# Moving loads ahead of waits in a fused mLSTM and mixture-of-experts kernel: SP's order, POOL's queue and the last three units' product

## The chip, the cores and the metric

The kernel runs on one core of a Trainium2 chip. The metric is the device time of one execution in microseconds; lower is better. The core has a matrix engine (PE, with its weight loads PEld), a vector engine (DVE), a scalar engine for activations (ACT), a general engine (POOL), and SP, which here only issues DMAs. All DMAs are issued by SP or by POOL, each from a queue in program order: an instruction that waits holds back everything behind it on the same engine.

## The reference

Part one is an mLSTM over 4 batches, 8 heads, 768 steps and head size 40. Part two routes its 3072 output rows of 320 to the best 2 of 8 experts.

```python
for t in range(S):
    m_new = np.maximum(f_gate[:, :, t] + m, i_gate[:, :, t])
    f_stab = np.exp(f_gate[:, :, t] + m - m_new)
    i_stab = np.exp(i_gate[:, :, t] - m_new)
    C = f_stab * C + i_stab * einsum('bhd,bhe->bhde', vt, kt)
    n = f_stab * n + i_stab * kt
    h_tilde = einsum('bhde,bhe->bhd', C, qt)
    denom = np.maximum(np.abs(einsum('bhd,bhd->bh', n, qt)), 1.0)
    y[:, :, t] = sigmoid(o_gate[:, :, t]) * h_tilde / denom
...
noisy = x @ w_gate + log1p(exp(x @ w_noise)) * noise      # 8 logits a row
top2_w = softmax over the two largest
out[row] += top2_w[row, k] * (relu(x[row] @ w1[e]) @ w2[e])    # for both choices
```

## The kernel before

**Units.** The recurrence is computed by chunks of 64 steps. A unit is one chunk of two batches, 128 rows of x; there are 24 (`NU`): 12 chunks of the first two batches, then 12 of the others. The `while i < NU` loop holds one iteration a unit, in which the steps of several units are interleaved. For unit `u`: `e_part` makes the decay matrix `w` (PE, then Exp on ACT) from gate operands `LE` and `RE`; `s_part` multiplies queries and keys; `p_part` and `k_part` (DVE) weigh them (`p`, `kd`); `c_part` makes the next state, `o_part` the output; `f_part` divides by the normaliser on DVE (`tm`) and multiplies by the output gate on POOL (`XR[u]`, "xr" in the profile: the unit's 128 rows of x). An iteration later `t_part` transposes `XR` on PE for the router's logits.

**Loads.** `load_unit(u, "k")` brings queries and keys (tile `qk`, four buffers), `load_unit(u, "v")` values, keys and output gates (`vk`, four buffers), both from SP. In iteration `i` they are for unit `i + 3`. Its `vk` buffer is that of unit `i - 1`, so the load waits until `XR[i - 1]`, its last reader, is done. `keep_rows(i - 1)` writes `XR[i - 1]` to a table `rows` (`XD`) in DRAM: from POOL up to unit 11, from SP after. `gate_move` copies gate values into `LE` and `RE` every other iteration, from POOL for `i < XV` and from SP after. `piece_w1` and `early_w2` bring the first expert's weights in pieces.

**Routing.** Every four units form a group. The generator `g_part` picks the two experts of each row, their weights and their places; `fill` deals its steps out between the steps of the units. ACT's share of it is issued by `act()` at fixed points (L648). The step at L517 takes a difference `d` on POOL, which ACT then exponentiates; L549 and L550 give the two weights (`WTS`). Then their DMA to `rows` is put on the list `sent`, and SP issues it at the top of the next iteration (L762), or in `push()` behind the loop (L844). When the first 16 units are ranked, `decode` (L441 to L445) finds the rows of the first expert's first 512 places and `gather` (L716) fetches them and their weights from `rows` with four indirect DMAs on POOL, in the last iteration.

**Experts.** Behind the loop `transpose_x` (L746 to L750) turns each gathered tile: PE transposes, ACT and DVE split it into a high and a low part. Then `mm1` (L887) and `mm2` (L905 to L907) run for the two parts of each expert, and `put` adds the result to the output by indirect DMA. The output is first filled with zeros by 16 DMAs of SP (`zeros`, L275), and the second expert's weights follow them on SP.

The order on each engine is that of the program; nothing reorders it.

Of the kernel before, what the change touches and what calls it, by code (L numbers as in the profile page):

```python
# [17 lines left out]
NE, F, DM = 8, 1024, 320  # L18
# [3 lines left out]
NU = 2 * NCH  # L22
# [20 lines left out]
RW = 336  # L43

XV = 13
GC = 2
VW = 968
KE = 98
# [7 lines left out]
def build(ctx, tc, qk, vk, fi, noise, wgn, w1, w2, cst, ce, out):  # L56
    nc = tc.nc
    V, A, P, T, SP = nc.vector, nc.scalar, nc.gpsimd, nc.tensor, nc.sync
# [8 lines left out]
    XD = dram.tile([NTOK, RW], F32, name="rows")  # L67
# [9 lines left out]
    WTS = keep.tile([128, NU, RW - DM], F32, name="wts")  # L77
# [13 lines left out]
    gates = eg.enter_context(tc.tile_pool(name="gates", bufs=1, side="right"))  # L91
    RE = [gates.tile([128, 2, H, GC * L], FR, name=f"re{i}") for i in range(2)]
    LE = [gates.tile([128, GC, 192], FR, name=f"le{i}") for i in range(2)]
    HL = gates.tile([64, 2, S], FR, name="hl")
# [6 lines left out]
    SG = [t[:, 0, 648:VW] for t in VKS]  # L101
# [38 lines left out]
    def load_unit(u, what="kv", q=None):  # L140
        pr, c = divmod(u, NCH)
        if "k" in what:
            for p in range(2):
                (q or SP).dma_start(QK[u % 4][64 * p:64 * p + D], qk[pr, c, p])
        if "v" in what:
            flat = VKS[u % 4].rearrange("p x c -> p (x c)")
            SP.dma_start(flat[0:64, 0:VW], vk[pr, c, 0])
            SP.dma_start(flat[64:128, 648:648 + VW], vk[pr, c, 1])
# [56 lines left out]

    GB = NCH // GC

    def gate_move(kk, q=(SP, SP)):
        pr, k = divmod(kk, GB)
        j = kk % 2  # L210
        src = HL[32 * pr:32 * pr + 32, :, k * GC * L:(k + 1) * GC * L].bitcast(F32)
        q[0].dma_start(LE[j][64:96, :, 64:128].bitcast(F32), src[:, 0].rearrange("r (c t) -> r c t", c=GC))
        for x in range(2):
            q[x].dma_start(RE[j][96 + x:97 + x].bitcast(F32), src[16 * x:16 * x + 16, 1])

    def operands(j, p, eng=None):
        if p is None:
            A.activation(LE[j][0:KE], cet[0:KE, None, E_L:E_L + 192].to_broadcast([KE, GC, 192]), AF.Copy)
        else:
# [64 lines left out]
    W, PP, KD, SQ, OQ, XR, LG, MG = {}, {}, {}, {}, {}, {}, {}, {}  # L284
# [43 lines left out]
    def k_part(u):  # L328
        if u % NCH < NCH - 1:
            KD[u] = wk.tile([128, 2, H, D], F32, name="kd")  # L330
            V.tensor_mul(KD[u], VKS[u % 4][:, :, 328:648].rearrange("p x (h d) -> p x h d", h=H),
                         W[u][:, :, :, L - 1:L].to_broadcast([128, 2, H, D]))
# [29 lines left out]
    def f_part(u, step):  # L362
        ps = OQ[u]
        dn = wk.tile([128, H], F32, name="dn")
        V.tensor_scalar(dn, ps[:, :, D], 1.0, None, op0=OP.max)
        step()
        V.scalar_tensor_tensor(dn, ps[:, :, D], -1.0, dn, op0=OP.mult, op1=OP.max)
        step()
        V.reciprocal(dn, dn)
        step()  # L370
        XR[u] = rt.tile([128, DM], F32, name="xr", bufs=3)
        tm = wk.tile([128, H, D], F32, name="tm")
        V.tensor_mul(tm, ps[:, :, 0:D], dn[:, :, None].to_broadcast([128, H, D]))  # L373
        P.tensor_mul(XR[u], tm.rearrange("p h d -> p (h d)"), SG[u % 4])  # L374

    def keep_rows(u):
        (P if u < XV - 1 else SP).dma_start(XD[128 * u:128 * u + 128, 0:DM], XR[u])

# [91 lines left out]
    def g_part(g):  # L470

        u0, nb = GROUPS[g]
# [43 lines left out]
        d = sm("d", [128, nb])  # L516
# [32 lines left out]
        V.reciprocal(wt[:, :, 0], dd)  # L549
        P.tensor_mul(wt[:, :, 1], d, wt[:, :, 0])  # L550
        yield
        sent.append((XD.rearrange("(u p) c -> p u c", p=128)[:, u0:u0 + nb, DM:RW], WTS[:, u0:u0 + nb]))
        while not asked[4]:
            yield "wait"
        rank = rk[:, 8:].rearrange("p (e u) -> p u e", e=NE)
# [60 lines left out]
    sent = []  # L616
# [105 lines left out]
    def early_w2(j, n):  # L722

        SP.dma_start(raw2[:, j:j + n], w2[0, 128 * j:128 * (j + n)].rearrange("(j p) c -> p j c", p=128))
# [32 lines left out]
    i = 0  # L757
    while i < NU:
        unit[0] = i
        spent[0] = 0.0  # L760
        while sent:
            SP.dma_start(*sent.pop())  # L762
        if 1 <= i and i + 3 < NU:
            load_unit(i + 3)
        if i:
            keep_rows(i - 1)
        if i == 0:
            k_part(1)
        if i % 2 == 0 and i and i // 2 + 2 < 2 * GB:
            gate_move(i // 2 + 2, (P, P) if i < XV else (SP, SP))  # L770

        if W1LD <= i < W1LD + 12 and i % 2 == 0:
            j = (i - W1LD) // 2
            piece_w1(0, 512 * (j // 3), j % 3)
        if W2AT <= i < W2AT + 4:
            early_w2(2 * (i - W2AT), 2)
        if i == 3:
            SP.dma_start(cs[:, C_TRI:], cst[:, C_TRI:])
        if i == 4:
            SP.dma_start(nzt, noise)  # L780
        if not begun and done[0] >= E0U[0]:
            decode(0, E0S[1] // 128)
            begun = 1
        if begun and late < len(tiles(0, 0)):
            n = 2 if i + 1 < NU else 4
            gather(0, 0, tiles(0, 0)[late:late + n])
            late += n
            begun = 2
        if i == 0:
            sig_part(0)  # L790
        if i == 6:
            constants()
            V.tensor_copy(tri, cs[:, C_TRI:C_TRI + 128])
            V.tensor_copy(ones, cs[:, C_ONE:C_ONE + 128])
        if i + 1 < NU:
            p_part(i + 1)
        fill(0.2, False)
        if i + 2 < NU:
            s_room(i + 2)
        c_part(i)  # L800
        o_room(i)
        o_part(i)
        if i + LEAD < NU:
            e_part(i + LEAD, (0,))
        f_part(i, (lambda: fill(0.15, False)) if i + 2 < NU else (lambda: None))
        act()
        t = l_part(i)
        w = r_part(t)
        b = None if w else b_part(t)
        if i:  # L810
            t_part(i - 1)
            tc_part(i - 1)
        lc_part(i, t, w)
        bc_part(t, b)
        if i + LEAD < NU:
            e_part(i + LEAD, (1,))
        if i + 2 < NU:
            s_part(i + 2)
        fill(SHARE - spent[0])
        act()  # L820
        if i + 1 < NU:
            sig_part(i + 1)
        if i + 2 < NU:
            k_part(i + 2)
        fill(SHARE - spent[0])
        act()
        if i < 5:

            for _ in range(4):
                next(gates2, None)  # L830
        if W1AT <= i < W1AT + 12 and i % 2 == 0:
            next(pre1)
        if 6 <= i < 13:
            P.memset(XG[:, i - 6], 0.0)
        route(i)
        i += 1
        if i == NU - LEAD:
            eg.close()
            m1 = ctx.enter_context(tc.tile_pool(name="m1", bufs=1, side="right", reuse_waits="tile"))
            XH = m1.tile([128, 3, NT], FR, name="xh")  # L840
            XL = m1.tile([128, 2, NT], FR, name="xl")
# [341 lines left out]
```

## Time and profile before

| what | value |
|---|---|
| median of 3 runs | 570.92 us (570.37, 570.92, 576.92) |
| the profiled execution's own time | 572.61 us |
| its span in the profile | 570.5 us |
| mean granted clock of PE | 0.969 |
| the 24 units | about 7 to 142 us |
| from the last unit to the first expert's first product | about 142 to 152 us |
| the eight experts | about 152 to 564 us |

The span runs from the first instruction to the last; the rest of the execution's time lies around it. Rows of the profile give the start (or a count), a duration, the engine and line, the operation with the tiles it writes and reads, and in square brackets how long the engine had been idle just before and what ended that. "SPq" is SP's queue.

### The profile page before, as it was taken

Reading aid. Unit: us, or ns where it says so; the run is one execution under the profiler, and the core shown is the slowest. Engines: PE = TensorE matmul, PEld = TensorE weight load, DVE = VectorE, ACT = ScalarE, POOL = GpSimd, SP = SyncE. Lnnn points to the kernel's source line nnn. Section 1 sums busy time; section 2 is a strip of 40 time slices with the busy share of each in tenths; the row PEclk is TensorE's granted clock in tenths of the full one; section 3 lists DMA queues with packets and bytes.
Section 4 is the critical chain, followed back from the end, with each engine's and each line's share of the span. In section 5 each row is a group of like instructions: output and inputs, shape, how many; then the busy total and the mean of one; then the engine's idle time right before and its main releaser. Section 6 shows DMA issues by size and latency. Waiting matters only on the chain.

```text
span 570.5 us, 13345 instructions
## 1 busy us (share of the span) xinstructions
PE 545.3 (96%) x5158; PEld 494.8 (87%) x5158; DVE 352.4 (62%) x937; ACT 254.9 (45%) x621; POOL 244.0 (43%) x336
## 2 busy tenths in 40 slices
PE   8799898999699999999999999999999999999995
PEld 3588787888479898998899899889989998998995
DVE  8889999998594386654563565466356545644511
ACT  6576778876241354522541442254145225414500
POOL 7446676533456546046224604532460453241043
PEclk9799899998699899999999999999999999999998
DMA  5887889795379365264326326432642543232023
GB/s 142 190 212 209 210 203 219 213 236 152 105 235 312 85 114 128 93 152 71 114 42 146 90 93 149 63 99 59 150 96 93 143 58 85 79 40 25 2 31 47
DMA packets 41060, 71.11 MB, mean 125 GB/s; under 512 B 8761, under 2 KB 30478, under 8 KB 40992
## 3 DMA queue, kind: packets, MB, share of 16 engines
q1 hardware_dynamic: 29632, 51.23, 31.8%
q0 software_dynamic: 11360, 18.98, 19.3%
q8 instruction: 42, 0.69, 0.5%
q14 instruction: 26, 0.21, 0.1%
HBM read 52.76 MB, written 17.73 MB: 124 GB/s over the span
## 4 chain that ended last, share of the span: by engine, by line
PE 80%; DVE 8%; DMA 5%; ACT 3%; issue 2%; POOL 1%; SPq 1%; POOLq 0%; DVEq 0%
PE s L887 22%; PE e L887 11%; PE st L907 5%; PE st L906 5%; PE st L905 5%; PE o L907 4%; PE o L906 4%; PE o L905 4%; PE s L746 3%; PE s L323 3%; DMA vk<-vk_in 2%; PE o L360 2%; PE e L298 2%; PE st L351 2%; PE xt L405 1%
## 5 line engine op out<-in xcount | busy, mean ns | idle before, releaser
L931 POOL DMA_INDIRECT y_out<-y,tok x56 | 87.1, 1556 | 220.5 <-DVE y L921 219.8
L887 PE MATMUL s<-xh,w1h 128*128 128x512 f32 (+1 forms) x255 | 78.0, 361 | 1.5 <-DVE xh L750 0.9
L893 DVE SCALAR_TENSOR_TENSOR hlo<-s,hh 128x512 fp32r<-128x512 f32 (+1 forms) x85 | 47.4, 558 | 41.2 <-ACT hh L892 36.7
L748 ACT ACTIVATE xh<-s 128x384 fp32r<-128x384 f32 (+1 forms) x56 | 25.4, 469 | 103.2 <-PE s L746 102.9
L716 POOL DMA_INDIRECT xg<-rows,tok x56 | 58.4, 1043 | 26.2 <-issue 16.8
L892 ACT ACTIVATE hh<-s 128x512 fp32r<-128x512 f32 (+1 forms) x85 | 41.7, 491 | 48.6 <-PE s L887 46.5
L887 PE MATMUL s<-xh,w1l 128*128 128x512 f32 (+1 forms) x255 | 63.1, 356 | 0.0
L905 PE MATMUL st<-w2h,hh 128*128 128x320 f32 x184 | 58.0, 315 | 0.0
L907 PE MATMUL st<-w2h,hlo 128*128 128x320 f32 x184 | 57.2, 311 | 0.0
L906 PE MATMUL st<-w2l,hh 128*128 128x320 f32 x184 | 56.8, 309 | 0.0
L887 PEld LDWEIGHTS s<-xh,w1h 128*128 128x128 f32 x255 | 46.2, 190 | 7.9 <-ACT xh L748 2.0
L905 PE MATMUL o<-w2h,hh 128*128 128x320 f32 x168 | 53.0, 315 | 0.0
L907 PE MATMUL o<-w2h,hlo 128*128 128x320 f32 x168 | 52.4, 312 | 0.0
L906 PE MATMUL o<-w2l,hh 128*128 128x320 f32 x168 | 51.9, 309 | 0.0
L887 PEld LDWEIGHTS s<-xh,w1l 128*128 128x128 f32 x255 | 45.1, 190 | 6.0
L887 PE MATMUL s<-xl,w1h 128*128 128x512 f32 (+1 forms) x170 | 46.6, 355 | 0.5 <-DVE xl L749 0.5
L374 POOL TENSOR_TENSOR xr<-tm,vk 128x320 f32<-128x320 f32 x24 | 22.2, 926 | 43.0 <-DVE tm L373 12.9
L887 PE MATMUL e<-xh,w1h 128*128 128x320 f32 (+1 forms) x129 | 39.7, 363 | 0.0
L749 DVE TENSOR_TENSOR xl<-s,xh 128x256 fp32r<-128x256 f32 (+1 forms) x56 | 22.6, 404 | 26.9 <-ACT xh L748 23.3
L323 PE MATMUL s<-qk 64*64 64x64 f32 x768 | 36.2, 233 | 0.7 <-issue 0.7
L921 DVE TENSOR_SCALAR y<-st,gw 128x320 f32<-128x320 f32 x23 | 12.7, 551 | 39.2 <-PE st L907 39.2
L893 DVE SCALAR_TENSOR_TENSOR hlo<-e,hh 128x256 fp32r<-128x256 f32 (+1 forms) x43 | 23.8, 554 | 18.8 <-ACT hh L892 17.9
(203 smaller groups left out, 1368.7 us busy)
## 6 DMA issues: line engine op xcount, KB each, us to landing
vk<-vk_in SPq DMA_DIRECT2D x48, 242.0 KB
raw<-w_in SPq DMA_DIRECT2D x7, 1280.0 KB
qk<-qk_in SPq DMA_DIRECT2D x48, 160.0 KB
raw<-w_in SPq DMA_DIRECT2D x7, 1024.0 KB
y_out<-zrow SPq DMA_DIRECT2D x15, 320.0 KB
raw<-w_in SPq DMA_DIRECT2D x18, 256.0 KB
rows<-xr POOLq DMA_DIRECT2D x12, 160.0 KB
rows<-xr SPq DMA_DIRECT2D x12, 160.0 KB
```

The source lines that it names most:

```text
L323: T.matmul(SQ[u][:, p][half[p], h, :], q[r, 1, h, :], q[r, 0, h, :], start=True, stop=True)
L374: P.tensor_mul(XR[u], tm.rearrange("p h d -> p (h d)"), SG[u % 4])
L716: P.indirect_dma_start(out=XG[0:rows_of(t), t], out_offset=None, in_=XD[0:n], in_offset=bass.IndirectOffsetOnAxis(ap=token(e, t), axis=0), ...
L748: A.activation(XH[:, :, c], ps[:, :, 0:n], AF.Copy)
L749: V.tensor_sub(XL[:, :, c], ps[:, 0:2, 0:n], XH[:, 0:2, c].bitcast(F32))
L887: T.matmul(ps[:, 0:n], l, r, start=i == 0, stop=i == len(ops) - 1)
L892: A.activation(HH[:, f, c], ps[:, 0:m], AF.Relu)
L893: V.scalar_tensor_tensor(HLO[:, f, c], ps[:, 0:m], 0.0, HH[:, f, c].bitcast(F32), op0=OP.max, op1=OP.subtract)
L905: T.matmul(ps, HH[:, j, c], W2H[:, j], start=j == 0, stop=False)
L906: T.matmul(ps, HH[:, j, c], W2L[:, j], start=False, stop=False)
L907: T.matmul(ps, HLO[:, j, c], W2H[:, j], start=False, stop=j == 7)
L931: st = P.indirect_dma_start(out=out, out_offset=bass.IndirectOffsetOnAxis(ap=token(e, t), axis=0), in_=y[0:n], in_offset=None, compute_op= ...
```

## The change

Three things are changed. In an iteration SP issues the queries and keys first, then gates and weight pieces, and only then the values and the kept rows, which wait for x; where gates and kept rows go by POOL, they change places in the same way. The two weights of a group go to `rows` from POOL, where they are computed, instead of from SP's list. And the product that makes x runs on DVE instead of POOL for units 21, 22 and 23.

```diff
+XP = 21
...
-        P.tensor_mul(XR[u], tm.rearrange("p h d -> p (h d)"), SG[u % 4])
+        (P if u < XP else V).tensor_mul(XR[u], tm.rearrange("p h d -> p (h d)"), SG[u % 4])
...
         yield
-        sent.append((XD.rearrange("(u p) c -> p u c", p=128)[:, u0:u0 + nb, DM:RW], WTS[:, u0:u0 + nb]))
+        P.dma_start(XD.rearrange("(u p) c -> p u c", p=128)[:, u0:u0 + nb, DM:RW], WTS[:, u0:u0 + nb])
...
         spent[0] = 0.0
-        while sent:
-            SP.dma_start(*sent.pop())
         if 1 <= i and i + 3 < NU:
-            load_unit(i + 3)
-        if i:
-            keep_rows(i - 1)
+            load_unit(i + 3, "k")
         if i == 0:
             k_part(1)
         if i % 2 == 0 and i and i // 2 + 2 < 2 * GB:
...
         if W2AT <= i < W2AT + 4:
             early_w2(2 * (i - W2AT), 2)
+
+        if 1 <= i and i + 3 < NU:
+            load_unit(i + 3, "v")
+        if i:
+            keep_rows(i - 1)
```

**SP in iteration 14** (`qk`, `vk`: loads of unit 17; `rows<-xr`: kept rows of unit 13; `le`, `re`: gates; `raw`: a piece of weights). Before:

```order
L144 DMA qk_99<-qk_in 40x1024 x2
L147 DMA vk_103<-vk_in 64x968
L148 DMA vk_103<-vk_in 64x968
L377 DMA rows<-xr 128x320
L212 DMA le_93<-hl 32x2x64
L214 DMA re_91<-hl 1x16x128 x2
L117 DMA raw_113<-w_in 128x512
```

Now:

```order
L146 DMA qk_99<-qk_in 40x1024 x2
L214 DMA le_93<-hl 32x2x64
L216 DMA re_91<-hl 1x16x128 x2
L119 DMA raw_113<-w_in 128x512
L149 DMA vk_103<-vk_in 64x968
L150 DMA vk_103<-vk_in 64x968
L379 DMA rows<-xr 128x320
```

Gates and weights moved ahead of the values; the queries are behind the kept rows of the iteration before in both.

**POOL at the end of the loop** (`wts`: the weights of the group of units 12 to 15; `xr`: x of a unit; `xg<-rows`: the four gathers; `d`: the difference of the next group's logits). Before:

```order
L550 TENSOR_TENSOR wts<-d_2451,wts 128x4
L374 TENSOR_TENSOR xr<-tm,vk_102 128x320
...
L374 TENSOR_TENSOR xr<-tm,vk_103 128x320
L374 TENSOR_TENSOR xr<-tm,vk_104 128x320
L435 TENSOR_TENSOR tbl<-tbl,share 128x56
L716 DMA xg<-rows,tok 128x336 x4
L374 TENSOR_TENSOR xr<-tm,vk_105 128x320
L517 TENSOR_TENSOR d_2864<-mx_2827 128x4
```

Now:

```order
L552 TENSOR_TENSOR wts<-d_2451,wts 128x4
L554 DMA rows<-wts 128x4x16
L376 TENSOR_TENSOR xr<-tm,vk_102 128x320
...
L437 TENSOR_TENSOR tbl<-tbl,share 128x56
L718 DMA xg<-rows,tok 128x336 x4
L519 TENSOR_TENSOR d_2864<-mx_2827 128x4
```

The DMA of the weights stands between the weights and x of unit 20, and the three products of units 21 to 23 are gone from around the gathers.

**SP behind the loop** (`rows<-xr`: kept rows of units 22 and 23, in the second list of unit 21 too; `y_out<-zrow`: zeros; `rows<-wts`: weights of the last two groups). Before:

```order
L377 DMA rows<-xr 128x320 x2
L275 DMA y_out<-zrow 128x2x320 x2
L844 DMA rows<-wts 128x4x16
L275 DMA y_out<-zrow 128x2x320 x10
L844 DMA rows<-wts 128x4x16
L275 DMA y_out<-zrow 128x2x320 x3
L275 DMA y_out<-zrow 128x320
```

Now:

```order
L379 DMA rows<-xr 128x320 x3
L277 DMA y_out<-zrow 128x2x320 x15
L277 DMA y_out<-zrow 128x320
```

The two DMAs of weights between the zeros are gone, and the zeros stand directly behind the kept rows.

## The prediction

> **What bounds the kernel now.** I read the head of the page first, then busy time by stretch, then the waits.
>
> ```profile
> PE 545.3 (96%) x5158; PEld 494.8 (87%) x5158; DVE 352.4 (62%) x937; ACT 254.9 (45%) x621; POOL 244.0 (43%) x336
> ```
>
> The matrix engine (PE) is busy 96% of the span, so only its idle time and its slow-clock time can be won. The stretches (busy us of PE, PEld, DVE, ACT, POOL, then PE's granted clock, DMA share, GB/s) show where that lies:
>
> ```profile
> 54.00:66.00 12.00, 9.61 (x199) 8.60 (x193) 11.59 (x38) 7.20 (x18) 7.18 (x16) 0.86 0.80 209
> 82.00:90.00 8.00, 6.58 (x174) 5.78 (x172) 7.60 (x28) 5.84 (x16) 6.58 (x16) 1.00 0.88 208
> 90.00:125.00 35.00, 34.22 (x768) 30.14 (x765) 33.26 (x109) 27.97 (x71) 15.90 (x25) 1.00 0.85 214
> 125.00:132.00 7.00, 5.99 (x121) 5.13 (x116) 6.67 (x20) 5.29 (x14) 4.01 (x11) 0.82 1.00 269
> 142.00:152.00 10.00, 5.18 (x26) 3.40 (x26) 6.08 (x37) 3.43 (x11) 5.68 (x8) 0.73 0.47 145
> 158.00:166.00 8.00, 8.00 (x44) 6.74 (x43) 7.19 (x37) 2.30 (x8) 3.04 (x8) 1.00 0.92 309
> 190.00:540.00 350.00, 349.69 (x2130) 326.56 (x2131) 192.09 (x447) 136.30 (x336) 129.20 (x144) 1.00 0.41 91
> ```
>
> From 190 us on PE idles 0.3 us in 350, so nothing there can move. In the 24 units PE idles 2.4 + 1.4 + 0.8 + 1.0 = 5.6 us over the four early rows. The largest hole, 4.8 us, is 142 to 152, between the last unit and the first expert. What PE waits for in the units is told by the waits (us in total, times, longest):
>
> ```profile
> ACT d L648 <- POOL d L517: 13.4, 6, 4.8
> ...
> PE e L298 <- ACT w L301: 5.5, 4, 2.4
> ...
> PE e L298 <- DMA qk<-qk_in: 2.8, 1, 2.8
> ```
>
> PE waits for ACT's `w`, and ACT stood waiting for POOL's `d` (the routing), six times. Only one PE wait in the units is for a load, the early one; no row has PE waiting for a `vk` load.
>
> **The change, part by part.**
>
> *SP's order: 0.* SP does wait for x:
>
> ```profile
> SPq L147 <- POOL xr L374: 18.0, 8, 4.1
> ```
>
> But what it then issues has slack. The tightest `vk` load is unit 16's, used by the `kd` product on DVE; the slowest landing that the chain shows is 6.55 us:
>
> ```profile
> 89.26 0.47 SPq L147 DMA_DIRECT2D vk<-vk_in  x1
> 99.09 0.97 DVE L331 TENSOR_TENSOR kd<-vk,w 128x640 f32<-128x640 f32 x1
> 115.00 6.55 DMA vk<-vk_in
> ...
> 121.63 3.14 DMA vk<-vk_in
> ```
>
> 89.26 + 6.55 = 95.8 against 99.09: 3.3 us to spare, so an earlier load wins nothing. The queries now stand ahead only of their own iteration's gates and weights; they remain behind the previous iteration's `vk` load and kept rows, which wait for x. What can be lost: gates and weights now stand ahead of `vk`, 0.67 + 2.02 + 0.58 us of issue by these rows:
>
> ```profile
> 95.78 0.67 SPq L212 DMA_DIRECT2D le<-hl  x1
> 96.56 2.02 SPq L214 DMA_DIRECT2D re<-hl  x2
> 98.63 0.58 SPq L117 DMA_DIRECT2D raw<-w_in  x1
> ```
>
> These 3.3 us lie partly in the time in which SP waited for x anyway; even in full they just use up the slack above. I take 0 (bounds: 5.6 gained, if all of PE's idle time in the units hung on loads; 1 lost).
>
> *POOL's order up to unit 12: -0.3.* Gates now go ahead of the kept rows. In iteration 6:
>
> ```profile
> 51.87 0.59 POOL L377 DMA_DIRECT2D rows<-xr  x1 [0.30 <-POOL xr L374]
> ...
> 54.03 0.97 POOL L264 MEMSET w1l<- 64x1024 f32 x1
> ...
> 56.51 0.39 POOL L834 MEMSET xg<- 128x336 f32 x1
> 54.13 2.80 DVE L486 TENSOR_SCALAR t<-ue 128x32 f32<-128x32 f32 x1
> ```
>
> DVE's 128x32 operation stood 2.80 us, until POOL's row of memsets ended (56.90 against 56.93). It is what ACT's next logarithm waits for, and with it PE in the row 54 to 66. The kept rows waited 0.30 us for x just ahead; gates, which need no x, fill that. So POOL's row ends 0.3 us earlier: -0.3 (bounds -0.3 and 0).
>
> *The choices' weights by POOL: 0.* Six DMAs of 128 x 4 pieces of 64 bytes. No row shows one on POOL. Nearest are the kept rows, 128 pieces, and the gathers, 128 rows by index (min/median/max ns):
>
> ```profile
> L377 POOL DMA_DIRECT2D rows<-xr x12: 587/606/634, 25.8 to 85.4; - x12
> L716 POOL DMA_INDIRECT xg<-rows,tok x56: 941/1002/1307, 143.1 to 475.7; - x56
> ```
>
> The lower end is 0.61 us; the upper, at the gather's cost per piece, 4 x 1.00 = 4.0 us. I take 1.0, nearer the plain DMA, which it is. In the units it stands ahead of x (`xr`), which PE transposes later:
>
> ```profile
> 87.64 0.22 POOL L550 TENSOR_TENSOR wts<-d,wts 128x4 f32<-128x4 f32 x1
> 87.80 0.87 POOL L374 TENSOR_TENSOR xr<-tm,vk 128x320 f32<-128x320 f32 x1
> 91.33 0.52 PE L385 MATMUL xt<-cs,xr 128*128 128x128 f32 x3
> ```
>
> x then ends at 87.86 + 0.3 (the wait as at L377) + 1.0 + 0.87 = 90.0 against 91.33: hidden, with 1.3 us left. Its `vk` load, the one at 89.26 above, slips by about 1.3 us of its 3.3.
>
> The Trainium skill, page "SBUF — State Buffer", section "SBUF: two separate sides", speaks against this part: a DMA from POOL has its descriptors written there, and these are locked out while DVE runs an operation that takes the port pair they share. By it I should expect some of the six to stretch. The twelve kept rows span 587 to 634 ns in a stage with DVE at 33.26 of 35 us, so for DMAs the trace does not bear it out. By it the sum would grow only through case C below, and it is why C is not smaller.
>
> *x of units 21 to 23 by DVE, and what that frees: -0.5.* One such product is half of a `kd` (0.97 us at 128x640, above), so about 0.5 us; POOL's row of 0.87 is the upper end. Unit 22's falls into the 1.67 us in which DVE waited for `ue`. Units 21's and 23's push back routing work that PE reaches over 1 us later: 0, and 1.5 if none were covered. DVE's wait and POOL's tail before:
>
> ```profile
> 141.44 0.27 DVE L486 TENSOR_SCALAR t<-ue 128x32 f32<-128x32 f32 x1 [1.67 <-ACT ue L648]
> 143.05 1.16 POOL L716 DMA_INDIRECT xg<-rows,tok  x1 [1.39 <-DVE dn L365]
> ...
> 147.19 1.00 POOL L716 DMA_INDIRECT xg<-rows,tok  x1 [0.30 <-issue]
> 148.21 0.87 POOL L374 TENSOR_TENSOR xr<-tm,vk 128x320 f32<-128x320 f32 x1
> 149.27 0.20 ACT L648 ACTIVATE d<-d 128x4 f32<-128x4 f32 x1 [4.84 <-POOL d L517]
> ```
>
> The gathers start no earlier: POOL idled 1.39 us before the first, until DVE was past the decode of the places. But `d` loses the 0.87 us product ahead of it, and ACT and DVE turn to the first three tiles 0.8 us sooner. PE starts when the fourth has landed and been split:
>
> ```profile
> 147.19 2.99 DMA xg<-rows,tok
> 152.62 0.29 DVE L750 TENSOR_TENSOR xh<-s,xh 64x128 fp32r<-64x128 f32 x1
> PE s L887 <- DVE xh L750: 0.9, 1, 0.9
> ```
>
> DVE, behind by three tiles, finished the fourth at 152.91; the 0.8 us takes off 0.5 until the fourth tile itself is the limit. So -0.5 (bounds -0.9 and 0).
>
> *What follows on SP: +2.5.* SP's last kept row waited for POOL's late x; behind it stand the zeros for the output, 320 KB each:
>
> ```profile
> 140.88 8.57 SPq L377 DMA_DIRECT2D rows<-xr  x2
> 149.50 0.96 SPq L275 DMA_DIRECT2D y_out<-zrow  x2
> ...
> 158.06 7.94 SPq L275 DMA_DIRECT2D y_out<-zrow  x10
> 143.39 0.49 DVE L373 TENSOR_TENSOR tm<-o,dn 128x320 f32<-128x320 f32 x1
> ```
>
> Now x of unit 23 is ready at 143.9 + 0.5 = 144.4, and the zeros start at about 144.8 instead of 149.5; the weights, which held them back until 158, are gone from SP too. They are issued every 0.48 us but take 320 KB / 309 GB/s = 1.06 us each, so they pile up just while gathers two to four (144.5 to 148.2) need the DMA engines. Before, these had them alone. When the fourth is handed over, 7 are out: 7 x 1.06 - 3.4 = 4.0 us of zeros lie ahead. Bounds: 0, and +4.0 if it waits behind all. The nearest rows are the two `vk` landings, 6.55 against 3.14 us, +3.4 for a crowded one. I take +2.5, nearer to that than to 0 because gathers go by another queue.
>
> **Sum:** -0.3 - 0.5 + 2.5 = **+1.7 us**. On the profiled execution's 572.61 (a span of 570.5 and 2.1 around it) that is 574.3. That execution lay 1.7 above the median of the runs, 570.92, so the forecast for the median is **572.6**.
>
> **Rivals.**
>
> *A: the engines take gathers and zeros in turn.* Then a gather waits for at most one zeros DMA, 1.06 us: -0.8 + 1.06 = +0.3, or 571.2. For it: the two kinds come by different queues. Against: a `vk` load took 6.55 us where POOL's queue held little. No row of this trace shows a gather against a deep SP queue. The Trainium skill states A as a rule: in "DMA: Bandwidth & Descriptors", section "Queues, rings and completion order", each DMA engine goes round between the queues that have work, packet by packet.
>
> *B: loads did bound the units* by some wait put down to another engine. Then the 5.6 us of PE's idle time go: about 565.3. For it: SP's 18.0 us of waits for x. Against: 3.3 us of slack at the tightest load, and PE's stalls end on ACT.
>
> *C: the weights are dear on POOL* (slower). At 4.0 us, x of unit 12 ends at 93.0 and PE's transpose waits 1.7 us. At most four units have this: 6.8, so 579.4. It decides from 2.3 us a DMA on. Against: the 606 ns of 128 pieces.
>
> *D: SP's queue is not freed.* Queries still stand behind the previous kept rows; that is in the 0 above.
>
> **How the numbers follow.** Forecast (571 to 575) 0.45; A 0.27; B 0.08; C 0.12; 0.08 for what I do not see. The range 568.8 to 577.0 holds the forecast, A, and the cheap half of C. A measurement of this kernel tells about 2% (11.4 us) from no change. No case reaches that for certain: faster 0.02, same 0.95, slower 0.03.
>
> **What would show it.** Right: zeros issued from about 145, the fourth gather landing past 151.5, `d` on ACT at 148.5, PE's first expert at 153 to 155, the units' end within 0.5 us of before. Wrong: the fourth gather landing near 150.2 (A or better); `rows<-wts` on POOL over 2.3 us with PE waiting at L385's transposes (C); PE's idle time in the units gone (B).

## The result, and the profile after

The changed kernel takes **577.97 us** (median of 20 runs, 575.52 to 583.6) against 571.41 for the kernel before (20 runs beside it): a ratio of **1.0144, 95% interval 1.0121 to 1.0167**. This ratio leaves out, as slow, six executions of the kernel before (576.55 us and up) and none of the kernel after, so it lies above the quotient of the two medians, 1.0115. The forecast was 572.6 with a range up to 577.0. The profiled execution took 577.95, a span of 576.1; before it was 572.61 and 570.5.

Busy time by stretch of the kernel after (busy us of PE, PEld, DVE, ACT, POOL, PE's granted clock, DMA share, GB/s):

```profile
79.93:83.34 3.41, 1.66 (x64) 1.48 (x55) 3.27 (x20) 0.32 (x1) 0.90 (x3) 1.00 0.92 222
83.34:90.16 6.82, 6.82 (x79) 6.09 (x80) 5.68 (x16) 5.04 (x14) 6.08 (x12) 0.50 0.68 186
...
127.72:131.13 3.41, 2.00 (x32) 1.66 (x28) 3.27 (x10) 2.77 (x7) 1.61 (x5) 1.00 0.92 240
131.13:137.95 6.82, 6.65 (x102) 5.75 (x103) 5.56 (x15) 3.41 (x10) 3.73 (x7) 0.50 0.66 182
```

The same view of the kernel before:

```profile
83.34:90.16 6.82, 5.40 (x135) 4.67 (x133) 6.45 (x19) 6.00 (x16) 6.08 (x15) 1.00 0.88 212
...
126.09:129.50 3.41, 2.41 (x34) 1.84 (x34) 3.21 (x9) 3.25 (x10) 1.11 (x4) 1.00 0.98 276
129.50:132.91 3.41, 3.40 (x74) 3.11 (x68) 3.34 (x10) 1.83 (x5) 2.87 (x6) 0.50 1.08 258
```

PE's idle share tells nothing here: it is busy 95% and 96%. The clock column does. Between 80 us and the end of the units, PE after runs at half clock for two stretches of 6.82 us (79 and 102 matmuls where the full-clock stretch of before has 135); before, there is one of 3.41 us at 129.5. Each of these stretches follows one in which PE stood idle for 1 us or more. What made PE idle in the kernel after stands in its timeline (start, us, engine, line, out<-in, and in brackets the idle time ahead with what ended it):

```profile
78.66 1.27 POOL L139 TENSOR_TENSOR w1l<-raw,w1h 128x512 fp32r<-128x512 f32 x1 [1.02 <-ACT w1h L138]
78.69 1.29 DVE L505 TENSOR_TENSOR ln<-ln,nzt 128x32 f32<-128x32 f32 x1
...
83.34 0.55 PE L362 MATMUL o<-vk,p 64*64 64x41 f32 x6 [1.76 <-DVE tm L375]
...
123.05 1.31 POOL L139 TENSOR_TENSOR w1l<-raw,w1h 64x512 fp32r<-64x512 f32 x1 [1.07 <-DMA rows<-xr]
123.25 1.16 DVE L508 TENSOR_TENSOR nl<-ln,lg 128x32 f32<-128x32 f32 x1
131.28 0.80 PE L300 MATMUL e<-re,le 98*128 98x512 f32 x1 [1.56 <-ACT w L303]
```

and in that of the kernel before:

```profile
79.36 0.19 DVE L503 TENSOR_TENSOR ln<-ln,nzt 128x32 f32<-128x32 f32 x1
79.59 0.19 DVE L506 TENSOR_TENSOR nl<-ln,lg 128x32 f32<-128x32 f32 x1
80.05 1.29 POOL L137 TENSOR_TENSOR w1l<-raw,w1h 128x512 fp32r<-128x512 f32 x1 [1.74 <-ACT w1h L136]
```

A small DVE row of the routing, 0.19 us before, takes 1.29 and 1.16 us after: it starts 0.03 and 0.20 us behind POOL's split of `w1` and ends with it (78.66 + 1.27 = 79.93; 78.69 + 1.29 = 79.98). Before, the two rows were through 0.27 us ahead of the split. I call this a **collision**. From the second one to PE's wait the link is `d`: ACT stands for it longer than before, and the `w` that PE waits for stands behind it.

```profile
128.26 0.21 ACT L650 ACTIVATE d<-d 128x4 f32<-128x4 f32 x1 [2.76 <-POOL d L519]
```

Before:

```profile
125.84 0.21 ACT L648 ACTIVATE d<-d 128x4 f32<-128x4 f32 x1 [1.85 <-POOL d L517]
```

DVE rows stand beside POOL's product x as well, in the kernel before too (0.7 to 1.2 us); those are not counted here.

The end of the units and the hand-off to the experts, of the kernel after:

```profile
144.34 1.13 PE L362 MATMUL o<-vk,p 104*64 104x41 f32 x32
...
148.70 14.87 SPq L277 DMA_DIRECT2D y_out<-zrow  x16
150.99 1.00 POOL L718 DMA_INDIRECT xg<-rows,tok  x1 [0.30 <-issue]
...
156.28 0.90 PE L748 MATMUL s<-cs,xg 128*128 128x128 f32 x3 [0.20 <-DMA xg<-rows,tok]
157.77 0.79 PE L890 MATMUL s<-xh,w1h 128*128 128x512 f32 x1 [0.58 <-ACT xh L750]
```

and the same matmuls of the last unit before:

```profile
140.51 1.13 PE L360 MATMUL o<-vk,p 104*64 104x41 f32 x32
```

The last unit's `o` matmuls start at 144.34 (before 140.51) and the first expert matmul at 157.77 (151.70). So of the 5.6 us of span, **3.8 arise in the units, 2.2 in the hand-off** (13.4 us against 11.2), and -0.4 behind it.

### The profile page after: what moved, and what is told of

Its sections match the earlier page's. It is cut to its first block, busy times and chain, and to the rows that moved or that the text cites. A ratio compares the mean times of both kernels' runs of the same rounds, so it can differ in the third digit from the quotient of the medians.

```text
span 576.1 us, 13332 instructions
## 1 busy us (share of the span) xinstructions
PE 546.1 (95%) x5158; PEld 495.7 (86%) x5158; DVE 357.7 (62%) x940; ACT 255.0 (44%) x621; POOL 246.3 (43%) x339
## 4 chain that ended last, share of the span: by engine, by line
PE 74%; DVE 12%; DMA 6%; ACT 3%; issue 2%; POOL 2%; SPq 1%; POOLq 0%; DVEq 0%
PE s L890 22%; PE e L890 10%; PE st L910 5%; PE st L909 5%; PE st L908 5%; PE o L910 4%; PE o L909 4%; PE o L908 4%; PE s L748 3%; DMA vk<-vk_in 2%; DVE p L339 2%; DVE ob L604 2%; PE s L325 1%; PE o L362 1%; PE o L916 1%
## 5 line engine op out<-in xcount | busy, mean ns | idle before, releaser
L376 POOL TENSOR_TENSOR xr<-tm,vk 128x320 f32<-128x320 f32 x21 | 21.0, 1000 | 36.0 <-DVE tm L375 13.8
L909 PEld LDWEIGHTS st<-w2l,hh 128*128 128x128 f32 x184 | 34.9, 189 | 0.0
```

The costliest lines, as they stand in the source:

```text
L376: (P if u < XP else V).tensor_mul(XR[u], tm.rearrange("p h d -> p (h d)"), SG[u % 4])
L909: T.matmul(ps, HH[:, j, c], W2L[:, j], start=False, stop=False)
```

## The experiments

Four marks are read from each profile, in us: the start of the last unit's `o` matmuls (**units' end**); PE's **half clock** from 80 us to there; the **gathers**, from POOL's first gather to PE's first expert matmul; and where a **collision** starts. The half clock ahead of 80 us is left out: besides a stretch in the first units, between 14 and 33 us, it is the one near the wait at 57 to 60 us that all kernels have, which was 3.4 to 13.7 us long behind the same code (3.4 in both before and after); so the units' end of one profile is good to some 5 us. Ratios are to the kernel before on the same chip.

| run | ratio (95%) | median us | units' end | half clock | gathers | collisions |
|---|---|---|---|---|---|---|
| before | 1 | 569.7 to 572.1 | 140.5 | 3.4 | 8.65 | none |
| after | 1.0144 (1.0121 to 1.0167) | 577.97 | 144.3 | 13.6 | 10.9 | 78.7, 123.3 |
| p1_order | 1.0066 (1.0014 to 1.0118) | 571.1 | 138.5 | 3.4 | 8.8 | none |
| p2_weights | 1.0179 (1.0097 to 1.026) | 578.3 | 145.0 | 10.2 | 8.5 | 121.9 |
| p3_x_dve | 1.0013 (0.9969 to 1.0058) | 570.0 | 137.9 | 0 | 9.5 | none |
| c1_weights_sp | 0.9993 (0.9944 to 1.0043) | 571.6 | 136.9 | 0 | 10.0 | none |
| a2_held | 1.011 (0.9987 to 1.0233) | 580.1 | 147.5 | 13.6 | 10.4 | 127.9 |
| c2_zeros_free | 0.9996 (0.9943 to 1.0049) | 570.7 | 137.3 | 0 | 9.7 | none |
| d3_free | 1.0015 (0.9973 to 1.0057) | 572.1 | 137.9 | 0 | 10.5 | none |
| d2_held | 1.0023 (0.9978 to 1.0067) | 570.2 | 141.2 | 0 | 8.5 | none |
| d1_behind | 1.0104 (1.0062 to 1.0147) | 578.4 | 144.2 | 13.6 | 8.6 | 78.7, 123.1 |
| d4_after_behind | 1.0159 (1.0083 to 1.0234) | 581.5 | 146.4 | 17.1 | 10.5 | 78.4, 123.4 |
| e2_dve_twice | 1.0048 (1.0011 to 1.0084) | 572.8 | 139.9 | 3.4 | 9.1 | none |
| e3_dve_else | 1.0162 (1.0114 to 1.0211) | 577.2 | 147.2 | 6.8 | 8.75 | 103.9 |
| f1_guard | 1.0115 (1.0063 to 1.0167) | 576.3 | 139.8 | 3.4 | 10.7 | none |
| f2_held_guard | 1.0002 (0.9969 to 1.0036) | 570.8 | 137.7 | 0 | 8.55 | none |

Four more runs move the splits and stand below.

### Each part alone

Order alone: the diff of the change from `load_unit(i + 3, "k")` on, with `sent` left in place.

> The kernel before with one part alone: in a unit SP and POOL get queries, gates and expert weights first, then the v rows and the kept rows; choices' weights stay on SP, x stays on POOL. Theory T (the units' +3.8 us are a matter of phase: the order shifts DVE's routing work against POOL's low parts of w1, a two-input DVE row then stands about 1.1 us behind a 1.28 us POOL row, PE runs dry and goes to half clock): the last unit's o matmuls start 2 to 5 us later than the 140.5 of before or about the 144.3 of after, with rows of 1.0 to 1.3 us at L503 or L506 beside the low parts at L137; time about +2 to +5 us. Rival R1 (the weights' DMA on POOL makes x late, and with it the routing): this part alone has no such DMA, so the units end at 138 to 140.5, the time is 0 to -2 us. Rival R2 (gates ahead of v rows make loads late): like T in time, but PE's or DVE's waits in units 11 to 13 and 20 to 22 end on vk loads. The hand-off (last o matmuls to PE's first expert matmul, 11.2 us before, 13.4 after) stays at 11.2 in all of them.

Weights alone:

```diff
-        sent.append((XD..., WTS[:, u0:u0 + nb]))
+        P.dma_start(XD..., WTS[:, u0:u0 + nb])
```

> The kernel before with one part alone: the choices' weights by POOL's queue. The DMA takes 0.8 to 0.85 us there as in the kernel after. Theory T: no change of order ahead of unit 8, so the early 2.2 us are not won; POOL's rows move by about 1 us from unit 8 on, a collision may come or go: -1 to +2 us in the units. Rival R1: the units lose 3 to 5 us, with PE waiting for transposes of x or for routing behind them. Hand-off: the last group's weights no longer stand ahead of the zeros on SP, but the zeros still wait for x of unit 23 on POOL (149 us): 11.2 us, or up to 12 if the zeros that follow without a pause reach the fourth gather.

x alone:

```diff
-        P.tensor_mul(XR[u], ...)
+        (P if u < 21 else V).tensor_mul(XR[u], ...)
```

> The kernel before with one part alone: x of units 21 to 23 by DVE. Units as before up to unit 21 (last o matmuls at 140.5, within 0.5 us). Hand-off: x of unit 23 about 4 us earlier, so two zeros DMAs start at about 145, and the rest still waits for the last group's weights on SP: theory T (zeros ahead of the gathers cost the hand-off 2.3 us when 7 or more are out): two zeros are 2.1 us of transfers issued ahead of three gathers, so 10.5 to 12 us; total -0.5 to +1 us. Rival R3 (the hand-off's loss comes from DVE's products and the changed order on POOL, not from zeros): 13 us or more, total +2 us.

x costs nothing that the comparison tells, the order 0.1 to 1.2%; **the weights alone bring a loss as large as the whole change's** (578.3). Theory T had put it on the order, and falls; R1 had the part right. In the timeline and the stretches of the run with the weights alone the link is the same as after:

```profile
121.88 1.27 POOL L137 TENSOR_TENSOR w1l<-raw,w1h 64x512 fp32r<-64x512 f32 x1 [1.01 <-DMA vk<-vk_in]
121.91 1.28 DVE L503 TENSOR_TENSOR ln<-ln,nzt 128x32 f32<-128x32 f32 x1
130.29 0.49 PE L298 MATMUL e<-re,le 98*128 98x512 f32 x1 [1.55 <-ACT w L301]
```

```profile
132.28:142.52 10.24, 10.22 (x165) 9.30 (x161) 7.63 (x19) 5.16 (x12) 2.69 (x6) 0.50 0.33 100
```

One collision, PE idle for 1.55 us instead of 1.00, and 10.24 us at half clock where before had 3.41. The extra 6.8 us at half speed are 3.4 us, and the longer wait 0.55: most of the 4.5 us by which its units end later than before's. That the longer wait made the stretch longer is not shown by one profile each.

### The weights undone in the changed kernel

```diff
-        P.dma_start(XD..., WTS[:, u0:u0 + nb])
+        sent.append((XD..., WTS[:, u0:u0 + nb]))
...
+        while sent:
+            SP.dma_start(*sent.pop())
```

> The kernel after with one part undone: the choices' weights go by SP again, as before. Theory W (formed from the parts alone: the weights' DMAs on POOL, 0.8 us each ahead of x, put DVE late; its routing rows then fall behind POOL's split of w1, PE runs dry, and the clock goes to half for multiples of 3.4 us): without them no DVE row at L505 or L508 over 0.3 us, half clock in the whole span 27 us as before (37.6 after), last o matmuls at 137.5 to 140.5 (144.3 after), hand-off 11 to 11.8 us since the last group's weights hold the zeros; time within 1.5 us of before. Rival Q (the parts cost together what none costs alone: the new order and x on DVE together): last o matmuls past 143, time +4 us or more.

As W expected, but for a hand-off of 12.6 us in place of 11 to 11.8 (two zeros stood ahead of the gathers); the parts do not cost more together. In its timeline DVE is through 0.4 us ahead of the split, PE's wait is 0.47 us, and there is no half clock from 80 us to the units' end:

```profile
118.57 0.19 DVE L508 TENSOR_TENSOR nl<-ln,lg 128x32 f32<-128x32 f32 x1
119.16 1.27 POOL L139 TENSOR_TENSOR w1l<-raw,w1h 64x512 fp32r<-64x512 f32 x1 [1.12 <-DMA rows<-xr]
125.63 0.49 PE L300 MATMUL e<-re,le 98*128 98x512 f32 x1 [0.47 <-ACT w L303]
```

### The zeros

> The kernel before with x of units 21 to 23 by DVE, and the weights of the last group alone by POOL, the other five groups' by SP. Its units are those of the run with x on DVE alone (last o matmuls 137.9, within 1.5), but nothing holds the zeros on SP after x. Theory Z (zeros ahead of the gathers): hand-off from the last o matmuls to the first expert matmul 13 to 13.8 us, against 11.0 to 11.5 where the zeros came late or only two came; fourth gather 5 us from its issue to the transpose; time +1.5 to +4 us against x on DVE alone. Rival R3 (the long hand-off comes with the weights' DMAs or the order of the units): 11 to 11.8 us.

> The kernel after, with the weights of the last group alone by SP again, so that they hold all but two zeros DMAs behind the hand-off; the other five groups' weights by POOL. Units as after (last o matmuls 143 to 145.5). Theory Z: hand-off 11 to 11.8 us in place of 13.4, time about 2 us under after (575 to 576.5). Rival R3: hand-off stays at 13 us or more, time as after.

Both edits (the weights of the last group alone by another queue than the rest) missed their aim: the group ahead of the last also comes behind the units. So c2 still had two zeros ahead of the fourth gather, a2 five. Done properly, with x of units 21 to 23 on DVE as in c2:

```diff
+        if u0 < 16:
             sent.append(w)
+        else:
+            P.dma_start(*w)
```

> The kernel before with x of units 21 to 23 by DVE, and the weights of the last two groups by POOL, which both come behind the units; in the earlier run only the last group's were, and those of the one ahead of it still held all but two zeros. Units as with x on DVE alone. Theory Z: five zeros or more ahead of the fourth gather, first gather to first expert matmul 10.4 to 11 us, time +1 us against x on DVE alone, 0 to +2.5 against before. Rival R3: 9.5 to 10 us as with two zeros.

and the opposite, no zeros ahead, again with x on DVE:

```diff
-        mm1(0, 0, f, wipe)
+        mm1(0, 0, f, wipe if f else lambda: None)
```

> The kernel before with x of units 21 to 23 by DVE, and no zeros asked for in the first of the eight steps, so that all of them stand behind a group's weights, which come at about 155 us. Theory Z: with no zeros ahead of the gathers the first gather to the first expert matmul takes 8.0 to 8.4 us (9.5 with two zeros, 8.65 in before, where x and its product stand ahead of the routing on POOL), time 1 us under x on DVE alone, -0.5 to -2 us against before. Rival R3 (DVE's product and POOL's order make the hand-off long, not the zeros): 9.5 us or more, no gain.

Over the runs of the table, the gathers' mark goes by the zeros issued before POOL is through with issuing the fourth gather: none, 8.5 to 9.1 us (eight runs); two, 9.5 to 10.0 (three); five, 10.4 to 10.9 (five). It does not go by who multiplies x or sends the weights, so theory Z stands and R3 falls. The fourth gather and its transposition in d3, then in d2, whose zeros start at 158.02:

```profile
141.78 14.74 SPq L275 DMA_DIRECT2D y_out<-zrow  x16
...
144.03 0.99 POOL L720 DMA_INDIRECT xg<-rows,tok  x1 [0.30 <-issue]
...
148.98 0.90 PE L750 MATMUL s<-cs,xg 128*128 128x128 f32 x3 [0.35 <-DMA xg<-rows,tok]
```

```profile
147.26 1.00 POOL L716 DMA_INDIRECT xg<-rows,tok  x1 [0.30 <-issue]
...
150.16 0.90 PE L746 MATMUL s<-cs,xg 128*128 128x128 f32 x3 [0.17 <-DMA xg<-rows,tok]
```

From issue to transposition it is 4.95 us with the zeros and 2.90 without.

In the total, neither differs from before by more than the comparison tells.

### Where the weights' DMA stands on POOL

The DMA behind the group's last small product on POOL, so that x no longer waits for it: on the kernel before (d1) and on the changed one (d4).

```diff
         P.tensor_mul(OVM[:, u0:u0 + nb, 2:4], wt, ov)
+        P.dma_start(XD..., WTS[:, u0:u0 + nb])
```

> The kernel before with the choices' weights by POOL, as in the run with that part alone (578.3 us, +8.5), but the DMA issued behind POOL's last small product of the group (L586 of before) in place of ahead of x. POOL has the same DMAs, x no longer waits for them. Theory X (the cost is x being 1.1 us late on POOL, so that DVE's routing rows stand until the late product of x ends): DVE's rows are stretched by 9.5 to 11 us in all between 56 and 146 us, as before (10.6; 12.2 with the DMA ahead of x), last o matmuls at 137 to 141 (145.0), time within 1.5% of nothing: -1 to +2 us against before. Rival P (any DMA of 0.8 us on POOL in a routing group costs as much, by what it keeps from POOL or by descriptors that shut DVE out): last o matmuls 143 to 146, time +5 us or more.

> The kernel after with the same move: the weights' DMAs behind the group's last small product on POOL, all else as after; the zeros on SP stay free. Theory X with theory Z: last o matmuls 136 to 140 (144.3 after), first gather to first expert matmul 10.4 to 11 us as after (10.9; 8.5 to 8.8 where no zeros stand ahead), time -1 to +2 us against before. Rival P: last o matmuls past 143, time +5 us.

X falls, P holds: 578.4 and 581.5. But the rows of d1's timeline are again a collision, and PE's waits are those of the kernel after to 0.01 us (1.76 and 1.56):

```profile
122.90 1.30 POOL L137 TENSOR_TENSOR w1l<-raw,w1h 64x512 fp32r<-64x512 f32 x1 [0.34 <-DMA vk<-vk_in]
123.09 1.15 DVE L506 TENSOR_TENSOR nl<-ln,lg 128x32 f32<-128x32 f32 x1
```

### The splits of w1 moved

`a1_odd`: all six in odd units; `c3_late_split`: ACT's and POOL's part of the second and sixth one unit later; `e1_low_late`: POOL's part alone of these two; `e4_held_low_late`: the same as e1, on d2, without weights on POOL.

```diff
-        if W1AT <= i < W1AT + 12 and i % 2 == 0:
+        if W1AT < i < W1AT + 12 and i % 2:                            # a1
+        if i in (8, 11, 12, 14, 16, 19):                              # c3
+        if W1AT <= i < W1AT + 12 and i % 2 == 0 or i in (11, 19):     # e1, e4
...
+                if lo is P and (f, k) in ((0, 1), (512, 2)):              # e1, e4
+                    yield
                 lo.tensor_sub(W1L[n, k, s], ...)
```

> The kernel after, with the six splits of w1 in odd units (9 to 19) in place of even ones (8 to 18); the routing's two-input DVE rows stand in even units. Theory T: no row at L505, L508 over 0.3 us, PE's stalls in units 12 to 13 and 21 shrink to those of before or less, no half-clock stretch at 84 to 90; the last o matmuls start at about 139 to 141.5 in place of 144.3, the time falls by 3 to 5 us against after, to about -1 to +4 us against before with the hand-off of 13.4 us unchanged. Rivals R1 and R2 (late x, late loads): the stalls stay, the last o matmuls start at 143.5 to 145, the time stays within 1 us of after's 576.4 to 578.

> The kernel after, with the second and the sixth split of w1 one unit later (units 8, 11, 12, 14, 16, 19 in place of 8, 10, 12, 14, 16, 18): the two that stood beside DVE's L505 at 78.7 us and L508 at 123.3. Theory W with the collision as its link: no such row over 0.3 us, PE's idle 1.76 us at L362 gone, half clock in the units 17 us down to 7 to 10, last o matmuls at 139 to 142 unless the moved splits meet other rows of DVE (over 0.6 us beside L139). Rival W2 (the weights' DMAs cost by x being late, the split has no part in it): last o matmuls stay at 143.5 or later.

> The kernel after, weights' DMAs and all, with POOL's low part of the second and the sixth piece of w1 one unit later (units 11 and 19), while ACT's high part stays where it was (the earlier run moved both, and put 0.61 us of ACT's work between d and w). Theory K (collision: the two-input routing rows of DVE stand behind the split): no row over 0.3 us at L505 or L508 of after, PE's idle before the o matmuls of unit 12 1.0 us or less (1.76), half clock in the units 10 us or less (17), last o matmuls at 137 to 141 (144.3), time -0.5 to +3 us against before with the hand-off of after. Rival P (the DMAs on POOL cost by themselves): last o matmuls past 143, time +5 us or more.

> The kernel before with x of units 21 to 23 by DVE, all zeros behind the weights (the run with the shortest hand-off), and POOL's low part of the second and the sixth piece of w1 one unit later. Theory K: fewer executions in which the rows collide, so fewer runs above 573 us (14 of 29 of before's last runs); median 568 to 570.5, -0.5 to -3 us against before. Rival (the upper runs of before have another cause): same share of runs above 573, median as before.

All four take longer than before: 1.0211 (1.0114 to 1.0307), 1.0181 (1.0082 to 1.028), 1.0135 (1.0086 to 1.0184), 1.0187 (1.0135 to 1.0238). e4 is the one to read first: d2 with nothing but two POOL rows moved, and 580.8 against 570.2. In all four the two rows of the routing keep their 0.19 us throughout, as K asked, and yet PE runs 20 to 27 us at half clock from 80 us to the units' end. So the loss can come without a collision; moving a split costs what it should save, and these runs do not tell what the collisions of the kernel after cost. In c3, ACT's 0.61 us of `w1h` got between `d` and the `w` that PE waits for, and PE waited 1.99 and 2.07 us. With the splits moved, the kernels with and without weights on POOL (e1 577.6, e4 580.8) do not stand apart the way p2 and before do.

### DVE made late with no DMA on POOL

The product `tm` written twice, in units 10 and 18 (e2), or in 12 and 20 as a control (e3):

```diff
+        for _ in range(2 if u in (10, 18) else 1):     # e3: (12, 20)
             V.tensor_mul(tm, ...)
```

> The kernel before, no DMA of weights on POOL, but DVE's product tm of units 10 and 18 is written twice, which makes DVE about 0.4 us later there. In before L503 and L506 of these units ended 0.27 us ahead of POOL's split in one and started 0.05 us ahead of it in the other. Theory K: L503 or L506 over 1 us beside L137 in one or both units, then PE idle of 1.5 us or more and half clock: last o matmuls at 142 to 146 (140.5), time +3 to +8 us for 0.8 us of work. Rival P: no DMA, so +0.8 us at most.

> Control: the same product written twice, in units 12 and 20 in place of 10 and 18, where no split of w1 stands beside the two-input routing rows. Theory K: no row over 0.3 us at L503 or L506, time 0 to +1 us. If being 0.4 us late costs DVE as much anywhere (theory L: DVE is simply the bound in the units): +3 us or more, as with units 10 and 18.

Both expectations of K missed, each by its place: e2 met no split and cost 0.5%; the control met one, in unit 14, and cost 1.6%. Its collision with the wait of PE that ended about then, and the half clock behind:

```profile
103.75 1.26 POOL L137 TENSOR_TENSOR w1l<-raw,w1h 128x512 fp32r<-128x512 f32 x1 [1.12 <-ACT w1h L136]
103.91 1.16 DVE L507 TENSOR_TENSOR nl<-ln,lg 128x32 f32<-128x32 f32 x1
...
104.54 0.33 PE L323 MATMUL s<-qk 64*64 64x64 f32 x2 [2.58 <-issue]
```

```profile
106.11:112.94 6.83, 6.81 (x88) 5.89 (x85) 4.75 (x22) 3.48 (x9) 1.99 (x4) 0.50 0.89 234
```

So a collision needs no DMA on POOL, and where 0.4 us of lateness ends in one could not be told from the rows of before. That this one cost the loss is not shown: PE stood idle from 101.96 to 104.54, from ahead of the collision until 0.53 us before its end, and what ended that wait the profile does not show. Besides, 13.7 us of half clock lay between 58 and 72 us already.

### The split made to wait

All in its place; ahead of each low part POOL copies 128x1 of `nl`, and so waits until DVE has written it: on the changed kernel (f1) and on d2 (f2).

```diff
+                if lo is P and NL:
+                    P.tensor_copy(gate, NL[-1][:, 0, 0:1])
                 lo.tensor_sub(W1L[n, k, s], ...)
...
         V.tensor_add(nl, ln, lg[:, :, 0:8])
         yield
+        NL.append(nl)
```

> The kernel after, with a 128x1 copy of the group's nl on POOL ahead of each low part of w1, so that the split waits until DVE has written nl (the L508 row of after), about 0.5 to 1.2 us, where it would otherwise start beside L501 to L508. Nothing else is moved. Theory K (collision): no row over 0.3 us at those lines, PE's idle of 1.76 and 1.56 us down to 1.0 or less, half clock in the units 10 us or less (17), last o matmuls 136 to 141 us (144.3), time 0 to +3 us against before, the hand-off's 2.2 us being left. Rival P (POOL's DMAs cost by the time they take there): gaps, half clock and time as after, +5 us or more; the copy adds about 0.1 us each.

> The kernel before with x of units 21 to 23 by DVE and all zeros behind the weights, and the same copy ahead of the splits. Theory K: no collision in any execution, so no loss from the copy and fewer of the executions above 573 us (5 of 12 without the copy): median 568.5 to 570.5. If the copy itself costs (POOL's split later, and with it what stands behind it): 572 or more, and then it is no neutral test above either.

f1's timeline:

```profile
78.76 0.18 POOL L142 COPY gate<-nl 128x1 f32<-128x1 f32 x1 [1.60 <-DVE nl L512]
78.90 1.27 POOL L143 TENSOR_TENSOR w1l<-raw,w1h 128x512 fp32r<-128x512 f32 x1
81.84 0.37 PE L366 MATMUL o<-vk,p 64*64 64x41 f32 x6 [0.73 <-DVE tm L379]
128.83 0.50 PE L304 MATMUL e<-re,le 98*128 98x512 f32 x1 [1.02 <-ACT w L307]
```

```profile
91.00:140.00 49.00, 47.00 (x1043) 41.48 (x1043) 45.97 (x145) 37.71 (x99) 22.64 (x39) 1.00 0.76 200
```

POOL stood idle until `nl` was written, 1.60 us (after, 1.02 until `w1h`). The collisions are gone with the DMAs still on POOL, PE's waits at these two places fell from 1.76 and 1.56 to 0.73 and 1.02, half clock behind 80 us from 13.6 to 3.4 (beside a wait of 1.41 us at 85.83, which before has too: 1.42 at 86.94), and the units end at 139.8 (144.3). **In the profiled execution this is what K said**, at 573.88 f1's fastest. **By the timed runs it is not:** the median of 576.3 is 5.0 us above before, past K's 0 to +3 and at rival P's price; it is 1.7 below that of after, and the two intervals (1.0063 to 1.0167 and 1.0121 to 1.0167) overlap.

A part of the rest stands in f1's timeline. A DVE row that began during the weights' DMA stood until the x behind it was done:

```profile
65.05 0.81 POOL L559 DMA_DIRECT2D rows<-wts  x1 [0.30 <-POOL wts L557]
65.59 1.20 DVE L586 TENSOR_SCALAR ai<-r 128x8 int32<-128x8 int32 x1
65.88 0.88 POOL L380 TENSOR_TENSOR xr<-tm,vk 128x320 f32<-128x320 f32 x1
```

In c1, without the DMA, this row took 0.17 us. Beside this x f1 has such a row in each of the four groups that fall into the units, 1.03 to 1.20 us; the longest that c1 has there are 0.54 to 0.83. The copy does not part this from the collision.

f2 shows that the copy costs nothing that the comparison tells. Executions above 573 us remain in it (3 of 12, against 5 of 12 in d2); none of them was profiled, so whether they hold collisions is not known.

**What is shown:** the loss in the units comes with the weights on POOL: it appears when they alone are moved there (p2, d1) and goes when they alone are moved back (c1). With the splits in place, the profiles of the six kernels 1.0% or more above before (a2's interval reaches 1), f1 apart, have a collision, and none of the eight within 1% of before has. From the `tm` of unit 10 to that of unit 23 these six take 71.2 to 73.8 us, before, the eight and f1 64.8 to 67.6. In four of the six half clock follows the collision by way of a wait of PE; in a2 it starts at 87 us, ahead of it, and in e3 the wait is not the collision's. Keeping the split back removed collision, waits and half clock in one profile. **What is argued:** that the collisions make the loss in the executions that were not profiled; f1's median speaks for a small part only. **What stays open:** why those of f1 still stand some 5 us above before, when its gathers explain about 2 and the rows beside x some more. No version beats the kernel before: c1, c2, p3, d2, d3 and f2 equal it.

## Why the prediction was wrong, point by point

- **The choices' weights by POOL: 0. This step failed.** The sum in it held: the DMA took 0.81 us (taken: 1.0), and x of unit 12 ended at 90.27, ahead of PE's transpose at 93.10. One reading was wrong: the twelve kept rows lie between 25.8 and 85.4 us, while the 33.26 of 35 us of DVE are the row from 90 to 125, so they say nothing of a DMA on POOL in that stretch.

```profile
88.56 0.81 POOL L554 DMA_DIRECT2D rows<-wts  x1 [0.29 <-DMA vk<-vk_in]
89.39 0.88 POOL L376 TENSOR_TENSOR xr<-tm,vk 128x320 f32<-128x320 f32 x1
93.10 0.53 PE L387 MATMUL xt<-cs,xr 128*128 128x128 f32 x3
```

  The step missed what followed. I asked only whether PE would wait for x. I did not ask which DVE rows the shifted POOL rows would now meet, though the prediction itself quoted DVE's 128x32 row standing 2.80 us behind POOL. The margins, 0.27 and 0.05 us, could be read in the trace of before: enough for a chance and a price, though not, as e2 and e3 show, for the unit that it would hit. In place of 0 the runs show +8.5 and +6.8 us in the medians of p2 and d1, and the profile of after +3.8 in the units. In the profiles it goes by the collisions, PE's waits behind them and half clock; how much of the medians does is open.
- **Rival C** had the sign and nearly the time (579.4), but not the mechanism: it needed 2.3 us a DMA, which took 0.81 to 0.85. That its price fits is luck. None of the prediction's signs of being wrong came; what came was not among its rivals. Of its signs of being right one failed, the units' end within 0.5 us of before.
- **SP's order: 0**, nearly right: alone it is 0.1 to 1.2% slower, yet c1, which has it too, equals before. PE's waits on loads all lie in the first 21 us: before, two for the queries (2.8 and 1.4 us, where the prediction counted one), after, 2.1 for the gates and 0.3 for queries; none in the units behind, in either. **Rival B** (loads bound the units) falls.
- **POOL's order: -0.3**, right at its place. The DVE row behind POOL's memsets took 2.80 before and 2.40 with the order alone (p1); in the timeline after:

```profile
52.97 2.41 DVE L488 TENSOR_SCALAR t<-ue 128x32 f32<-128x32 f32 x1
```

- **x by DVE: -0.5**, about right: the product took 0.49 us. With no zeros in the way (d2, f2) units' end to first expert matmul is 10.5 us against 11.2, -0.7; not by `d` but by a first gather 0.55 us earlier.
- **The zeros: +2.5**, right in its size, partly by luck. With -0.5 the forecast for the hand-off was +2.0; it is +2.2. Zeros were issued from 148.7 on while the gathers were out, and the fourth was transposed 5.3 us after its issue (before 3.0), 2.3 later. But five zeros were issued by the time the fourth was handed over, 3.3 us after the first of them, not seven. Worked as in the prediction that is an estimate of 5 x 1.06 - 3.3 = 2.0 us of zeros ahead: the gather was late by about all of them, where the forecast took a part of a longer row. **Rival A** (in turn, at most one zeros DMA) falls: 2.3 us is over twice 1.06. By the Trainium skill, "DMA: Bandwidth & Descriptors", section "Queues, rings and completion order", on which A drew, the engines go round between the queues packet by packet; that this keeps the wait to one DMA was A's reading, and these rows do not agree with it.
- **The range**, to 577.0, held half of C and no loss by way of the clock: in p2's profile PE's wait is 0.55 us longer than before's, and the half clock behind it costs 3.4 us more.

## What to carry to other kernels

When work is added to an engine off the critical path, look for which rows of its neighbours it will newly stand beside, and read the margins to those rows; a delay that hides from its reader can still shift another pair into each other. Price a PE wait with the half-clock stretch that may follow it, not by its own length. Where one profile shows the cure and the timed runs do not, believe the timed runs. Before a part is judged by a moved one, run the move alone: here the cure cost as much as the illness.

## What the runs showed of the hardware

- **A small DVE row waits for the end of POOL's row.** 0.19 us became 1.15 to 1.29 when it began 0.03 to 0.2 us behind a POOL split, in six kernels; begun 0.05 us ahead of it, it kept its 0.19, as in the timeline of before below. The Trainium skill, "SBUF — State Buffer", section "Who interferes with whom", says so of DVE rows with two SBUF inputs against POOL rows that read SBUF, the later one standing until the earlier is done; these rows agree.

```profile
121.79 0.19 DVE L506 TENSOR_TENSOR nl<-ln,lg 128x32 f32<-128x32 f32 x1
...
121.84 1.28 POOL L137 TENSOR_TENSOR w1l<-raw,w1h 64x512 fp32r<-64x512 f32 x1 [1.31 <-DMA re<-hl]
```

- **Half clock comes in pieces of 3.41 us on a fixed grid.** Its starts in the kernel after, 59.44, 83.34 and 131.12, lie 7 and 14 pieces apart. The Trainium skill, "TensorE: Matmul & The Clock Gate", section "Part 1: The HAM clock gate", has a free-running window of 3413 ns, which agrees, and half clock after at least one idle window, which does not, if an idle window is one without work: PE was busy for half of the piece ahead of the fall at 83.34 (1.66 of 3.41), and in e4 for three quarters. Nor does busy time decide alone, nor does one busy piece bring the full clock back: from 83.34 to 90.16 PE was busy throughout two pieces at half clock. First e4's stretches, then d2's:

```profile
87.02:90.44 3.42, 2.64 (x58) 2.31 (x52) 3.32 (x10) 2.23 (x6) 2.97 (x5) 1.00 0.37 93
90.44:104.09 13.65, 12.92 (x188) 11.26 (x190) 10.85 (x28) 7.54 (x20) 8.14 (x16) 0.50 0.78 196
```

```profile
87.79:91.20 3.41, 2.58 (x75) 2.19 (x77) 3.12 (x12) 3.28 (x10) 3.23 (x7) 1.00 0.90 223
91.20:104.85 13.65, 12.46 (x273) 11.18 (x270) 13.17 (x43) 10.53 (x26) 6.28 (x9) 1.00 0.78 196
```

  With 2.64 of 3.42 us busy the clock fell for four pieces; with 2.58 of 3.41 it stayed. What tips it is not settled here.
